# Decay attention and GELU MLP in one kernel: a second v buffer and a single g buffer, early w_out loads, batch 1 in the row-tiled order

## The chip, the cores and the metric

One NeuronCore of a Trainium2 chip. The metric is the device time of one execution in microseconds (us). A kernel's figure is the median of its runs. A run more than 1.5% above the fastest of the same kernel counts as slow; ratios are of fast runs alone. The profile covers one of them; its span, from first to last instruction, is some 2 us shorter. Runs on one core carry the granted TensorE clock beside the time, as a share of full speed.

## The reference, cut to what matters

```python
def _attn_ref(q, k, v, f):                       # (8, 8, 576, 64), f: (8, 8, 576)
    scores = (1 / sqrt(64)) * q @ k^T
    cum = cumsum(log(clip(f, 1e-4, 1)))          # along the sequence
    scores = where(causal, -1e9, scores + cum[q] - cum[k])
    return softmax(scores) @ v
def _moe_ref(x, w_in, w_out):                    # x: (4608, 512), w_in: (512, 2048), w_out: (2048, 512)
    return gelu_exact(x @ w_in) @ w_out
```

The attention of eight batches, heads joined to 512 columns, then a two-layer MLP. The decay is applied as a weight on v, so TensorE sees plain attention.

## The kernel before: the parts that matter

The kernel works batch by batch: attention of batch b, with the second GEMM of batch b-1 filled in between its steps, then the first GEMM and Gelu of batch b. The 64 tail rows of each batch are gathered and go through the MLP at the end. Cuts are marked `...`.

```python
v_sb = consts.tile([P, H, NBLK, D], FP32)                            # v as loaded: one buffer
g_pool = ...(name="g", bufs=2)                                       # g: 16 tiles of 128 x 512 bf16 per batch
s_psum, o_psum, m_psum = ... # bufs=2 each: scores (2 banks a tile), attention outputs, GEMM outputs

def gemm1(c, ffb):
    ps = m_psum.tile(...)
    ...                                   # 4 matmuls of 128 x 512
    nc.scalar.activation(g_of[c][ffb], ps, Act.Gelu)

def transposes_pe(b, i, pool):            # q and k of one head pair: 12 transpositions on TensorE,
    ...                                   # into two banks of the pool, then 8 copies on VectorE

def x_tail_dma(b):                        # a DMA transposition on SyncE's queue
    nc.sync.dma_start_transpose(tails[...], xt_of[b][D:P]...)

for b in range(B):
    ...                                   # attention of b
    if b == 0:
        load_w_out(0)
        x_tail_dma(0)
    for ffb in range(n_ff):
        gemm1(b, ffb)
        if b == 0:
            if ffb in (6, 8, 13):
                transposes_pe(1, (6, 8, 13).index(ffb), s_psum if ffb < 10 else o_psum)
            if ffb == 9:
                weigh_v(1, 0)             # GpSimd; waits for v of batch 1
                for c in range(1, 4): load_w_out(c)
                load_qk_tokens(2); weigh_v(1, 1)
        ...
```

v has one buffer, so batch 1's v loads wait for batch 0's weighting. The batch-1 attention runs the second GEMM of batch 0 with full 128-row matmuls; the later batches split most of them into two row tiles of 64 (`gemm2_rows`), the mode in which the scores run too.

The softmax here doesn't subtract the row's maximum and nothing guards it: scores larger than these inputs give would overflow.

Of the kernel before, what the change touches and what calls it, by code (L numbers as in the profile page):

```python
# [50 lines left out]
def kernel(  # L51
# [30 lines left out]
    xT_pool = ctx.enter_context(tc.tile_pool(name="xT", bufs=2))  # L82
    g_pool = ctx.enter_context(tc.tile_pool(name="g", bufs=2))
    o_pool = ctx.enter_context(tc.tile_pool(name="outs", bufs=4))
# [21 lines left out]

    v_sb = consts.tile([P, H, NBLK, D], FP32)

    def load_v(b, h0=0, h1=H):
        if b >= B:  # L110
            return
        for n in range(NBLK):
            p0 = D if n == NBLK - 1 else 0
            nc.sync.dma_start(  # L114
                v_sb[p0:P, h0:h1, n, :],
                v[b, h0:h1, K0[n] + p0 : K0[n] + P].rearrange("h p d -> p h d"),
            )
# [18 lines left out]
    )  # L136
    nc.gpsimd.memset(v_sb[:, :, 0, 0:1], 0.0)
    load_v(0, 0, 4)
    load_qk_tokens(0, 6, 8)
    load_v(0, 4, 8)  # L140
    ident_fp = consts.tile([P, P], FP32)
    make_identity(nc, ident_fp)
# [29 lines left out]
    nc.scalar.activation(lf, f_sb, Act.Ln)  # L172
    nc.vector.memset(v_sb[0:D, :, 4, :], 0.0)
    nc.vector.tensor_tensor_scan(cum, ones, lf, 0.0, Alu.mult, Alu.add)
    nc.scalar.activation(wk, cum, Act.Exp, bias=cum[:, S // 2 : S // 2 + 1], scale=-1.0)

    def warm_up(n):
# [94 lines left out]
    def weigh_v(b, i):  # L272

        if b not in vw_of:
# [5 lines left out]
            vw_of[b][:, hs, :, 0:D],  # L280
            v_sb[:, hs, :, :],
            w.unsqueeze(3).to_broadcast([P, 2, NBLK, D]),
# [6 lines left out]
    def scores(b, i, t):  # L289
        on_pe = b == 0 or (b == 1 and i == 0)  # L290
        st = s_psum.tile([P, 2, 512], FP32, tag="s", name=f"s{t}")
# [166 lines left out]

    def gemm2_rows(c):




        for ts, steps in enumerate(STEPS):
            if ts < n_sub - 1:
# [35 lines left out]
    def first_attention():  # L501
# [29 lines left out]
        transposes(3, m_psum, "m")  # L531
        scores(0, 1, 3)
        weigh_v(0, 0)
        load_w_in(0)
        load_w_in(1)
# [5 lines left out]
        load_w_in(3)  # L541
        nc.gpsimd.memset(v_sb[:, :, 0, 0:1], 0.0)
        load_v(1, 0, 4)
        load_v(1, 4, 8)
        load_qk_tokens(1, 4, 8)
        scores(0, 2, 0)
        attend_head(0, 0)
# [22 lines left out]
    FILL_AV = [2, 1, 2, 2]  # L570
    FILL_1 = [[0, 4, 4, 0], [0, 2, 3, 3], [4, 4, 4, 4], [3, 3, 3, 3], [8, 0, 99]]

# [36 lines left out]
    def second_attention():  # L609
        b, fill, counts = 1, gemm2(0, True), FILL_1  # L610
        for i in range(HP):
            for t in range(4):
                scores(b, i, t)
                if i and t == 1:
                    attend(b, i - 1, 0, (0, 1, 2))
                elif i and t == 2:
                    attend(b, i - 1, 0, (3, 4))
                    normalize(b, i - 1, 0)
                elif i and t == 3:
                    attend(b, i - 1, 1, (0, 1, 2, 3, 4))  # L620
                    normalize(b, i - 1, 1)
                    if i < HP - 1:
                        x_dma(b, i - 1)
                if (i, t) == (0, 2):
                    transposes_pe(1, 3, o_psum)
                if i == 1 and t in (0, 2):
                    weigh_v(1, 2 + t // 2)
                if t == 3:
                    if i == 1:
                        load_v(2, 0, 4)  # L630
                    if i == 2:
                        transpose_dma(2, 0, 4)
                take(fill, counts[i][t])
        i = HP - 1
        take(fill, counts[HP][0])
        to_xT(b, i - 1, nc.vector.tensor_copy, o_psum, "o")
        attend(b, i, 0, (0, 1, 2, 3, 4))
        normalize(b, i, 0)
        take(fill, counts[HP][1])
        attend(b, i, 1, (0, 1, 2, 3, 4))  # L640
        normalize(b, i, 1)
        take(fill, 7)
        to_xT(b, i, nc.vector.tensor_copy, o_psum, "o")
        x_tail_dma(b)
        transpose_dma(2, 4, 8)
        load_v(2, 4, 8)
        take(fill, 999)

    for b in range(B):
# [6 lines left out]
        if b == 0:  # L656
            load_w_out(0)
            x_tail_dma(0)
        for ffb in range(n_ff):
            gemm1(b, ffb)  # L660
            if b == 0:
                if ffb in (6, 8, 13):
                    transposes_pe(
                        1, (6, 8, 13).index(ffb), s_psum if ffb < 10 else o_psum
                    )
                if ffb == 9:
                    weigh_v(1, 0)
                    for c in range(1, 4):
                        load_w_out(c)
                    load_qk_tokens(2)  # L670
                    weigh_v(1, 1)
            elif b + 1 < B:
                if ffb % 4 == 0:
                    untangle(b + 1, ffb // 4)
                if ffb % 4 == 2:
                    weigh_v(b + 1, ffb // 4)
                if ffb == 14:
                    load_qk_tokens(b + 2)
# [34 lines left out]
```

## Time and profile before

| what | before |
|---|---|
| median of runs | 353.1 us first; 352.7 to 353.9 beside the later runs |
| profiled span, granted clock | 350.2 us, 1.000 |
| TensorE busy | 338.7 us, 97% |
| batch 0's first GEMM begins | 27.83 us |
| batch 1's attention | 43.46 to 70.90 us |
| each of batches 3 to 7, first GEMM to next first GEMM | 36.58 us, (290.77 - 107.85) / 5 |

The main lines stand in the prediction. One view that it did not show belongs beside them: ScalarE around the end of a later batch's attention, from the timeline (start, duration, engine, line, operation; in brackets how long the engine idled before it and what ended that).

```profile
138.63 1.51 ACT L311 ACTIVATE e<-s 128x896 bf16<-128x896 f32 x2 [1.07 <-PE s L296]
140.16 1.28 ACT L404 ACT_TABLE_LOAD   x1
145.41 0.60 ACT L404 ACTIVATE g<-ps 128x512 bf16<-128x512 f32 x1 [3.96 <-PE ps L392]
```

The Gelu table is loaded the moment the last Exp is done, 4 us before the first Gelu has input. The load costs nothing. Nothing in a list of costs by duration says so: it is the same 1.28 us wherever it runs.

### The profile page before, as it was taken

To read this page: it belongs to the slowest core of one execution; us is meant where nothing else is said; L and a number is where in the kernel's file an instruction comes from. 1 tells how busy PE (TensorE), PEld (TensorE's weight loads), DVE (VectorE), ACT (ScalarE), POOL (GpSimd) and SP (SyncE) were. 2 spreads that over 40 slices of the span, in tenths; PEclk is the share of its full clock that TensorE was granted. 3 is DMA by queue.
4 is the path that set the end of the run, shared out by engine and by line. 5 is a ranking of instruction groups with operands and counts; after the bars stand their busy time and mean duration, and the time that the engine had idled before them with its cause. 6 is when DMAs were issued, how large, how long until landed. Compare 5 with 4: busy or idle time off the path is not lost.

```text
span 350.2 us, 7729 instructions
## 1 busy us (share of the span) xinstructions
PE 338.7 (97%) x3082; PEld 174.8 (50%) x3082; DVE 203.0 (58%) x499; ACT 216.1 (62%) x298; POOL 124.5 (36%) x243
## 2 busy tenths in 40 slices
PE   8998989999999999999999999999999999999995
PEld 3564534544555455545554455445544554444443
DVE  4561984496469935894579557956696563011011
ACT  5877585457874687468746874687567774603600
POOL 8291185415538044613453245514350530000000
PEclk9999999999999999999999999999999999999999
DMA  7999989974994998298928794679510131011013
GB/s 108 181 176 196 199 143 195 214 175 95 206 163 136 136 206 156 85 135 137 220 76 128 143 196 99 104 135 213 126 37 2 47 85 45 0 62 60 0 32 90
DMA packets 101219, 43.24 MB, mean 123 GB/s; under 512 B 80000, under 2 KB 96640, under 8 KB 101184
## 3 DMA queue, kind: packets, MB, share of 16 engines
q1 hardware_dynamic: 83888, 28.60, 40.1%
q0 software_dynamic: 16896, 13.63, 26.0%
q8 instruction: 24, 0.39, 0.5%
q10 hardware_dynamic: 400, 0.52, 0.4%
q14 instruction: 11, 0.09, 0.1%
HBM read 36.85 MB, written 9.44 MB: 132 GB/s over the span
## 4 chain that ended last, share of the span: by engine, by line
PE 83%; ACT 9%; POOL 2%; issue 2%; DMA 2%; SPq 1%; DVE 0%; ACTq 0%; POOLq 0%
PE ps L392 36%; PE ps L479 18%; PE ps L430 12%; PE o L332 9%; PE s L296 7%; ACT e L311 5%; ACT L311 2%; DMA v_sb<-in_v_dram 2%; ACT g L404 1%; POOL vw L279 1%; PE ps_x L368 1%; SPq L114 1%; POOL k L102 1%; POOL q L102 0%; PE s L305 0%
## 5 line engine op out<-in xcount | busy, mean ns | idle before, releaser
L404 ACT ACTIVATE g<-ps 128x512 bf16<-128x512 f32 x144 | 86.0, 597 | 82.2 <-PE ps L392 82.2
L311 ACT ACTIVATE e<-s 128x896 bf16<-128x896 f32 (+1 forms) x128 | 103.9, 862 | 30.7 <-PE s L296 25.5
L392 PE MATMUL ps<-xT,w_in_sb 128*128 128x512 bf16 x512 | 112.6, 379 | 0.7 <-ACT xT L371 0.6
L479 PE MATMUL ps<-w_out_sb,g 64*128 64x512 bf16 (+1 forms) x690 | 102.4, 376 | 0.0
L313 POOL TENSOR_SCALAR_AFFINE_SELECT e<-e 128x256 bf16<-128x256 bf16 x135 | 53.4, 406 | 113.5 <-ACT e L311 112.5
L392 PEld LDWEIGHTS <-w_in_sb 128*128 128x128 bf16 x576 | 56.0, 98 | 68.1 <-issue 2.9
L279 POOL TENSOR_TENSOR vw<-v_sb,wT 128x640 bf16<-128x640 f32 x32 | 41.0, 1280 | 47.5 <-DMA v_sb<-in_v_dram 15.8
L296 PE MATMUL s<-qT,kT 64*128 64x320 bf16 (+4 forms) x384 | 47.9, 282 | 4.0 <-ACT e L311 3.4
L479 PEld LDWEIGHTS <-g 64*128 64x128 bf16 (+1 forms) x690 | 37.7, 94 | 25.4 <-issue 1.6
L263 DVE COPY qT<-tq 64x288 bf16<-64x288 bf16 x96 | 45.1, 470 | 1.5
L332 PEld LDWEIGHTS <-e 128*128 128x128 bf16 x960 | 35.9, 98 | 17.6 <-issue 11.5
L430 PE MATMUL ps<-w_out_sb,g 128*128 128x512 bf16 (+2 forms) x208 | 44.3, 363 | 0.0
L332 PE MATMUL o<-vw,e 128*128 128x65 bf16 x960 | 41.7, 194 | 0.8 <-ACT e L311 0.4
L487 DVE COPY ot<-ps 128x512 f32<-128x512 f32 x24 | 16.5, 689 | 36.0 <-PE ps L479 36.0
L439 DVE COPY ot<-ps 128x512 f32<-128x512 f32 (+2 forms) x13 | 8.4, 650 | 48.9 <-PE ps L430 48.7
L296 PEld LDWEIGHTS <-kT 64*128 64x128 bf16 x384 | 20.1, 94 | 28.7 <-issue 15.6
L263 DVE COPY kT<-tk 64x288 bf16<-64x288 bf16 x96 | 32.3, 336 | 1.6
L347 DVE RECIPROCAL r<-o 128x5 f32<-128x5 f32 x64 | 12.5, 195 | 30.1 <-PE o L332 29.3
L348 DVE TENSOR_TENSOR x<-o,r 128x256 bf16<-128x256 f32 x64 | 27.2, 425 | 2.2
L430 PEld LDWEIGHTS <-g 128*128 128x128 bf16 x208 | 18.8, 98 | 18.9 <-issue 0.4
L358 DVE TENSOR_SCALAR xt<-o,r 64x64 bf16<-64x64 f32 x60 | 17.4, 290 | 1.4
L489 DVE TENSOR_TENSOR ot<-ot,ps 128x512 f32<-128x512 f32 x24 | 16.5, 687 | 1.3
(60 smaller groups left out, 144.7 us busy)
## 6 DMA issues: line engine op xcount, KB each, us to landing
out_dram<-ot SPq DMA_DIRECT2D x32, 256.0 KB, 2.4
v_sb<-in_v_dram SPq DMA_DIRECT2D x20, 256.0 KB, 4.6
v_sb<-in_v_dram SPq DMA_DIRECT2D x29, 128.0 KB, 5.5
q<-in_q_dram POOLq DMA_DIRECT2D x6, 576.0 KB, 6.5
k<-in_k_dram POOLq DMA_DIRECT2D x6, 576.0 KB, 8.6
w_in_sb<-in_moe_w_in_dram POOLq DMA_DIRECT2D x4, 512.0 KB, 7.9
w_out_sb<-in_moe_w_out_dram POOLq DMA_DIRECT2D x4, 512.0 KB, 9.3
q<-in_q_dram POOLq DMA_DIRECT2D x4, 144.0 KB, 4.4
```

Source lines behind the costliest of these rows:

```text
L263: nc.vector.tensor_copy(rows[:, odd], src[odd * D : (odd + 1) * D, 2 * i + h].rearrange("d j p -> d p j"),)
L279: nc.gpsimd.tensor_tensor(vw_of[b][:, hs, :, 0:D], v_sb[:, hs, :, :], w.unsqueeze(3).to_broadcast([P, 2, NBLK, D]), Alu.mult,)
L296: nc.tensor.matmul(st[:, h, c : c + w], kT[i][d, K0[n] : K0[n] + P], qT[i][d, q0 : q0 + w], start=True, stop=not on_pe or c not in SDIAG[t],)
L311: nc.scalar.activation(et[:, :, 0:c], st[:, :, 0:c], Act.Exp, scale=scale)
L313: nc.gpsimd.affine_select(out=et[:, :, c0 : c0 + P], in_=et[:, :, c0 : c0 + P], compare_op=Alu.is_ge, fill=0.0, base=0, pattern=[[0, 2], [ ...
L332: nc.tensor.matmul(o[:, m, :], e_of[b, i, t][:, h, c : c + P], vw_of[b][:, 2 * i + h, n, :], start=(n == 0), stop=(n == m),)
L348: nc.vector.tensor_tensor(x_of[b, i][:, :, h, :], o[:, 0:4, 0:D], r[:, 0:4].unsqueeze(2).to_broadcast([P, NBLK - 1, D]), Alu.mult,)
L358: nc.vector.tensor_scalar(*tail, r[D:P, 4:5], None, Alu.mult)
L392: nc.tensor.matmul(ps, w_in_sb[:, kt, ffb * P : (ffb + 1) * P], src[:, kt, :], start=(kt == 0), stop=(kt == n_dm - 1),)
L404: nc.scalar.activation(g_of[c][ffb], ps, Act.Gelu)
L430: nc.tensor.matmul(pss[ts][:, c0:c1], g_of[c][kt][:, ts * P : (ts + 1) * P], w_out_sb[:, kt, c0:c1], start=(kt == 0), stop=(kt == n_ff - 1),)
L479: nc.tensor.matmul(banks[r], g_of[c][kt][rows, ts * P : (ts + 1) * P], w_out_sb[rows, kt, :], start=(kt == 0), stop=last if r else kt == n ...
```

## The change

Its intent: batch 1's v comes early, so that GpSimd no longer holds w_out back behind a v wait; batch 1's attention takes the steady order as far as w_out's arrival allows; its causal masks move from TensorE to GpSimd. g goes from two buffers to one, presumably to make room for the second v buffer. The core of the diff:

```diff
-    g_pool = ctx.enter_context(tc.tile_pool(name="g", bufs=2))
+    g_pool = ctx.enter_context(tc.tile_pool(name="g", bufs=1))
-    v_sb = consts.tile([P, H, NBLK, D], FP32)
+    v_of = [consts.tile([P, H, NBLK, D], FP32, name=f"v_sb{i}") for i in range(2)]
     ...
     load_v(0, 4, 8)
+    load_v(1, 0, 4)
+    load_v(1, 4, 8)
     ...
-        on_pe = b == 0 or (b == 1 and i == 0)          # masks by TensorE
+        on_pe = b == 0
     ...
+    def gemm2_first(c):     # token blocks 0 and 1 full-row, by quarters of w_out
+        ...
+        yield from gemm2_rows(c, 2)
     ...
+        gate = x_pool.tile([P, 1], FP32, tag="gate", name="gate")
+        nc.gpsimd.tensor_copy(gate, v_of[0][:, 0, 2, 0:1])
+        load_w_in(0)
         weigh_v(0, 0)
-        load_w_in(0)
         ...
         load_qk_tokens(1, 4, 8)
+        for c in range(4):
+            load_w_out(c)
     ...
-    FILL_1 = [[0, 4, 4, 0], [0, 2, 3, 3], [4, 4, 4, 4], [3, 3, 3, 3], [8, 0, 99]]
+    FILL_1 = [[2, 2, 2, 2], [2, 2, 3, 3], [2, 3, 4, 4], [2, 3, 4, 4], [8]]
     ...                     # second_attention() rewritten in the form of attention()
-            load_w_out(0)
             ...
-                if ffb in (6, 8, 13):
+                if ffb in (6, 8, 12, 14):               # fourth pair here, no longer inside the attention
                 ...
-                    for c in range(1, 4):
-                        load_w_out(c)
+                    weigh_v(1, 1)
                     load_qk_tokens(2)
```

More of the change, by code (lines that the diff above doesn't have):

```diff
@@ L114, in load_v @@
             nc.sync.dma_start(
-                v_sb[p0:P, h0:h1, n, :],
+                v_of[b % 2][p0:P, h0:h1, n, :],
                 v[b, h0:h1, K0[n] + p0 : K0[n] + P].rearrange("h p d -> p h d"),
@@ L136 @@
     )
-    nc.gpsimd.memset(v_sb[:, :, 0, 0:1], 0.0)
+    nc.gpsimd.memset(v_of[0][:, :, 0, 0:1], 0.0)
     load_v(0, 0, 4)
@@ L172 @@
     nc.scalar.activation(lf, f_sb, Act.Ln)
-    nc.vector.memset(v_sb[0:D, :, 4, :], 0.0)
+    nc.vector.memset(v_of[0][0:D, :, 4, :], 0.0)
     nc.vector.tensor_tensor_scan(cum, ones, lf, 0.0, Alu.mult, Alu.add)
     nc.scalar.activation(wk, cum, Act.Exp, bias=cum[:, S // 2 : S // 2 + 1], scale=-1.0)
+    nc.vector.memset(v_of[1][0:D, :, 4, :], 0.0)
     def warm_up(n):
@@ L280, in weigh_v @@
             vw_of[b][:, hs, :, 0:D],
-            v_sb[:, hs, :, :],
+            v_of[b % 2][:, hs, :, :],
             w.unsqueeze(3).to_broadcast([P, 2, NBLK, D]),
@@ L457, with gemm2_rows @@
     ]
-    def gemm2_rows(c):
-        for ts, steps in enumerate(STEPS):
+    def gemm2_first(c):
+        pss = [
+            m_psum.tile([P, d_model], FP32, tag="m", name="ps2") for _ in range(2)
+        ]
+        for kq in range(4):
+            for ts in range(2):
+                for kt in range(4 * kq, 4 * kq + 4):
+                    nc.tensor.matmul(
+                        pss[ts],
+                        g_of[c][kt][:, ts * P : (ts + 1) * P],
+                        w_out_sb[:, kt, :],
+                        start=(kt == 0),
+                        stop=(kt == n_ff - 1),
+                    )
+                    if kt == n_ff - 1:
+                        ot = o_pool.tile([P, d_model], FP32, tag="ot", name="ot")
+                        nc.vector.tensor_copy(ot, pss[ts])
+                        nc.sync.dma_start(
+                            out[c * S + ts * P : c * S + (ts + 1) * P, :], ot
+                        )
+                    yield
+        yield from gemm2_rows(c, 2)
+    def gemm2_rows(c, ts0=0):
+        for ts in range(ts0, n_sub):
+            steps = STEPS[ts]
             if ts < n_sub - 1:
@@ L541, in first_attention @@
         load_w_in(3)
-        nc.gpsimd.memset(v_sb[:, :, 0, 0:1], 0.0)
-        load_v(1, 0, 4)
-        load_v(1, 4, 8)
         load_qk_tokens(1, 4, 8)
+        for c in range(4):
+            load_w_out(c)
         scores(0, 2, 0)
@@ L609, in second_attention, with av @@
     def second_attention():
-        b, fill, counts = 1, gemm2(0, True), FILL_1
+        fill = gemm2_first(0)
+        def av(i):
+            for h in range(2):
+                attend(1, i, h, (0, 1, 2, 3, 4))
+                if h == 0:
+                    take(fill, FILL_AV[i])
+                normalize(1, i, h)
         for i in range(HP):
             for t in range(4):
-                scores(b, i, t)
+                scores(1, i, t)
+                take(fill, FILL_1[i][t])
                 if i and t == 1:
-                    attend(b, i - 1, 0, (0, 1, 2))
-                elif i and t == 2:
-                    attend(b, i - 1, 0, (3, 4))
-                    normalize(b, i - 1, 0)
-                elif i and t == 3:
-                    attend(b, i - 1, 1, (0, 1, 2, 3, 4))
-                    normalize(b, i - 1, 1)
-                    if i < HP - 1:
-                        x_dma(b, i - 1)
-                if (i, t) == (0, 2):
-                    transposes_pe(1, 3, o_psum)
-                if i == 1 and t in (0, 2):
-                    weigh_v(1, 2 + t // 2)
-                if t == 3:
-                    if i == 1:
-                        load_v(2, 0, 4)
-                    if i == 2:
-                        transpose_dma(2, 0, 4)
-                take(fill, counts[i][t])
-        i = HP - 1
-        take(fill, counts[HP][0])
-        to_xT(b, i - 1, nc.vector.tensor_copy, o_psum, "o")
-        attend(b, i, 0, (0, 1, 2, 3, 4))
-        normalize(b, i, 0)
-        take(fill, counts[HP][1])
-        attend(b, i, 1, (0, 1, 2, 3, 4))
-        normalize(b, i, 1)
-        take(fill, 7)
-        to_xT(b, i, nc.vector.tensor_copy, o_psum, "o")
-        x_tail_dma(b)
+                    av(i - 1)
+                    if i < HP - 1:
+                        x_dma(1, i - 1)
+                if (i, t) in ((1, 2), (2, 0)):
+                    weigh_v(1, i + 1)
+                if (i, t) == (1, 3):
+                    load_v(2)
+                if (i, t) == (2, 3):
+                    transpose_dma(2, 0, 4)
+        take(fill, FILL_1[HP][0])
+        to_xT(1, HP - 2, nc.vector.tensor_copy, o_psum, "o")
+        av(HP - 1)
+        take(fill, 5)
+        to_xT(1, HP - 1, nc.vector.tensor_copy, o_psum, "o")
+        x_tail_dma(1)
         transpose_dma(2, 4, 8)
-        load_v(2, 4, 8)
         take(fill, 999)
@@ L661 @@
             if b == 0:
-                if ffb in (6, 8, 13):
+                if ffb in (6, 8, 12, 14):
                     transposes_pe(
-                        1, (6, 8, 13).index(ffb), s_psum if ffb < 10 else o_psum
+                        1, (6, 8, 12, 14).index(ffb), s_psum if ffb < 10 else o_psum
                     )
@@ L667 @@
                     weigh_v(1, 0)
-                    for c in range(1, 4):
-                        load_w_out(c)
+                    weigh_v(1, 1)
                     load_qk_tokens(2)
-                    weigh_v(1, 1)
             elif b + 1 < B:
```

## The prediction

> **What bounds the kernel now**
>
> I read the clock first (1.000 throughout, so no throttling confuses the times), then the page's busy shares and slices, then the chain of waits, then the busy time of each engine by stage, and last the order of instructions in the two stages that the change edits.
>
> ```profile
> PE 338.7 (97%) x3082; PEld 174.8 (50%) x3082; DVE 203.0 (58%) x499; ACT 216.1 (62%) x298; POOL 124.5 (36%) x243
> ...
> PE 83%; ACT 9%; POOL 2%; issue 2%; DMA 2%; SPq 1%; DVE 0%; ACTq 0%; POOLq 0%
> ```
>
> TensorE sets the time, from the first matmul to the last: 97% busy and 83% of the chain. A change can win only by taking matmul time, mode switches or TensorE waits out. The next lines, the busy time by stage, show where those are (columns: stretch, its length, then busy time and count of each engine).
>
> ```profile
> 27.83:42.30 14.47, 14.45 (x96) 7.30 (x96) 7.29 (x16) 9.61 (x15) 0.00 (x0) 1.00 1.23 201
> 42.30:47.65 5.35, 4.39 (x41) 2.16 (x40) 4.28 (x10) 4.38 (x6) 4.86 (x7) 1.00 0.58 104
> ...
> 47.65:70.90 23.25, 22.62 (x233) 10.83 (x231) 13.82 (x37) 12.71 (x15) 13.08 (x26) 1.00 1.12 197
> 84.95:107.69 22.74, 22.44 (x292) 12.96 (x289) 11.83 (x33) 16.02 (x19) 9.15 (x21) 1.00 1.07 187
> 121.68:144.34 22.66, 22.36 (x288) 12.87 (x288) 12.45 (x35) 16.06 (x19) 9.14 (x21) 1.00 0.81 158
> ```
>
> Batch 1's attention, which the change rewrites, runs from 43.46 (its first score matmul) to 70.90 us (the first matmul of the next first GEMM): 27.4 us. Batches 2 to 7 do the same work in 22.7. So at most 27.4 - 22.7 = 4.7 us is to be had there, 1.3% of 353.1.
>
> The timeline of TensorE, VectorE and GpSimd in the stage ahead shows two queues that matter:
>
> ```profile
> 34.77 1.96 DVE L232 COPY qT<-s_t 64x288 bf16<-64x288 bf16 x4 [7.08 <-PE s_t L220]
> 36.74 1.98 DVE L232 COPY kT<-s_t 64x288 bf16<-64x288 bf16 x4
> 38.75 1.96 DVE L232 COPY qT<-s_t 64x288 bf16<-64x288 bf16 x4
> 40.72 1.97 DVE L232 COPY kT<-s_t 64x288 bf16<-64x288 bf16 x4
> 42.72 1.97 DVE L232 COPY qT<-ps_t 64x288 bf16<-64x288 bf16 x4
> 44.71 1.95 DVE L232 COPY kT<-ps_t 64x288 bf16<-64x288 bf16 x4
> ```
> ```profile
> 42.79 1.28 POOL L279 TENSOR_TENSOR vw<-v_sb,wT 128x640 bf16<-128x640 f32 x1 [15.65 <-PE ps L392]
> 44.02 0.22 POOL L285 CAST vw<-wT 128x10 bf16<-128x10 f32 x1
> 44.16 2.31 POOL L159 DMA_DIRECT2D w_out_sb<-in_moe_w_out_dram x3
> ```
>
> First, each TensorE transposition of a head pair costs VectorE eight copies, 3.95 us, and from 34.77 to 46.66 VectorE does them back to back: it is the bound of that job. Second, GpSimd sits 15.65 us in front of batch 1's first v weighting, and the other three quarters of w_out queue behind it. The label names a matmul, but the last v load of batch 1 was issued at about 30.8 and landed 11.7 us later, 42.5, so I read this as a wait for v. It is why 42.30 to 47.65 has a DMA share of only 0.58.
>
> **What the Trainium skill says**
>
> - "PSUM — Partial Sum Buffer", Engine vs sequencer instructions: matmuls start and complete in program order. The trace agrees (nothing overtakes the 0.96 us wait at 46.71), and it is what turns a full buffer in front of one transposition into idle time for the first GEMM behind it.
> - "TensorEngine Tiling (Array Packing)", Key Properties: changing the tiling mode drains TensorE. The trace agrees: the score tile at 49.98 needs 0.30 us until the full-row matmul after it, though its 448 columns per head stream in 448/2.4 GHz = 0.187, and four full-row matmuls at 47.64, 0.86 of streaming, take 0.96 until the next scores. About 0.11 + 0.10 = 0.21 us a round trip.
> - "DMA: Bandwidth & Descriptors", Queues, rings and completion order: every DMA engine takes turns between the queues that have work. So the second v load competes with w_in. The trace shows about 200 GB/s when full, and a hole at 16 to 18 us (46 GB/s) that the v load can fill.
> - "TensorE: Matmul & The Clock Gate", What's actually happening: after about 3.4 us of idle TensorE falls to half clock. No such idle occurs in this trace.
>
> **The change part by part**
>
> 1. *Front.* The v load of batch 1 goes out right behind batch 0's, and w_in's first quarter is issued before, not after, the first weighting. That weighting starts at 15.00 when the last v chunk lands (8.84 + 6.00). The new gate waits for chunk 2, issued 7.74, landing about 6.1 later, 13.8; plus 0.8 of issuing is 14.7, so 15.00 stays. Only one w_in issue (0.78) now stands ahead of the second weighting, which TensorE waits 0.28 us for at 19.46. Gain 0.3.
>
> 2. *DMA.* From 16 us on, up to w_out's end, 2.1 MB of w_in (as written, bf16), 1.2 of q and k, 1.2 of v and 2.1 of w_out are left, 6.6 MB at 200 GB/s = 33 us, so the last quarter of w_out lands near 49, the first near 41. The first token blocks need quarter 0 in the first head pair, quarter 1 in the second: no wait. The later quarters of w_in land near 31 and 34 and are needed at 34.7 and 38 or later: no wait either. So the v wait of 15.65 us and the DMA hole vanish, but both were on GpSimd, off the path of TensorE, because the old fill counts already stepped around them.
>
> 3. *The fourth transposition.* It moves from the attention, where TensorE ran it at 47.13, into the first GEMM behind block 14. The third moves from block 13 to 12. Both use the two-bank pool of attention outputs, two tiles each. So the fourth has no free bank until VectorE has copied the third's q, at 42.72 + 1.97 = 44.69, and its k, at 46.66. VectorE's work has not changed, so neither have these times. TensorE finishes block 14 at 27.83 + 15 x 0.864 + 3 x 0.51 = 42.3. In order, it then waits till 44.69, does 0.26, waits till 46.66, does 0.26, and only then runs block 15, 0.86. The attention starts at about 47.9 in place of 43.46: +4.4, of which 0.5 is the transposition itself and 3.9 is new idle time.
>
> 4. *Batch 1's attention.* Removed: ten mask matmuls of the first pair, 10 x 128/2.4 = 0.53, and the transposition, 0.51. The masks become five GpSimd selects of 0.41; GpSimd was idle between its steps there, so they cost nothing on the path. Kept full-row: the 32 matmuls of two token blocks. The fill counts put them into the first three pairs, so 12 score tiles still pay 0.21 round trips; the steady order pays about two there. TensorE's busy time then is the steady 22.36 + 0.22 (a second transposition of x to xT) + 10 x 0.21 = 24.7. New waits: the first pair has only 2 fills a tile (0.43 us) where the steady batch has 6, 5, 4, 3. In the steady batch the first Exp ends 2.97 us after the attention's start (Gelu 0.60, table load 1.28, Exp 0.93); the third score tile needs its bank, while two tiles with four fills last 1.5. Counting on to the sixth tile gives about 1.2 us idle. And the third block wants both banks of the GEMM pool at once, one of which VectorE (0.69 a copy) has only just been handed: up to 0.8, taken as 0.4. Sum 24.7 + 1.2 + 0.4 = 26.3 against 27.4: -1.1.
>
> 5. *Single g buffer.* The Gelus of a batch overwrite g after the second GEMM has read it, all in TensorE's own order: 0. *Double v buffer in batches 2 to 7*: GpSimd's waits there are off the path (22.7 us a batch stays): 0.
>
> Sum: -0.3 + 4.4 - 1.1 = +3.0, 353.1 + 3.0 = 356.1 us.
>
> **The rivals**
>
> - *The stall hardly exists*, because VectorE starts earlier or empties the banks faster. Against it: 24 copies without a gap, 0.49 each. For it: a trial order that stalled so plainly would be odd to keep. Then only the transposition's 0.5 is added, and the time is 353.1 - 0.3 + 0.5 - 1.1 = 352.2; with the full steady gain in the attention, 349.
> - *The stall drops TensorE's clock.* Idle 2.4 and 1.7 us, with only 0.26 of work between, is near the skill's 3.4. Half clock for 3.4 to 7 us would cost 1.7 to 3.5 more: 358 to 360. Against it: two idles, neither alone that long.
> - *DMA contention moves the front.* If the v load and the earlier w_in delay batch 0's v or batch 1's q and k, GpSimd's first weighting slips past 15.00 and everything with it, one for one; 1 to 2 us, so 357 to 358. For it: the DMA engines are full from 8 to 14 us. Against: the second v load is behind the first in the same queue.
> - *The wait for w_out was dearer than I think*, so that ungating brings all 4.7 us: with the stall, 353.1 - 0.3 + 4.4 - 4.7 = 352.5. Against: TensorE idled only about 1.6 us in the whole old stage.
>
> **Range and chances**
>
> The rivals run from 349 to 360, with the weight near 356; the stall rests on a measured queue, the attention's sum on my counting of switches (plus or minus 1). I predict 356.1, 352.0 to 359.5. Two per cent is 7.06 us: faster than 346.0 needs more than the whole batch-1 excess, so 3%; slower than 360.2 needs stall and clock loss together, 6%; the rest, 91%, is within 2%.
>
> **What would show it right or wrong**
>
> Right: TensorE idle about 2.4 and 1.7 us behind block 14, released by VectorE's copies of the third pair; the first GEMM of batch 0 ending near 47.6 (from 43.46); batch 1's attention 26 to 27 us from there; the first w_out matmul never waiting for a DMA; batches 2 to 7 still 36.6 us each. Wrong: no gap there, VectorE copies far from 34.8 to 50.6, a granted clock under 1, the first weighting later than 15.3, or an attention under 25 us.

## The result

The changed kernel took 369.75 us (368.68 to 371.08, four runs) against 353.56 us for the kernel before: slower, ratio 1.0448 with a 95% interval of 1.0374 to 1.0521. Ratios here are the mean time of one kernel's fast runs over that of the other's in the same rounds, so not quite the quotient of the medians quoted. The profiled run of the changed kernel is its longest, 371.08 us, with a mean granted clock of 0.986. The other three had 0.991 to 0.995, so the profile shows more lost clock than the median run had.

The changed kernel's page first: busy shares, the clock in 40 slices, and the chain of waits by engine.

```profile
PE 342.5 (93%) x3052; PEld 174.7 (47%) x3094; DVE 204.9 (56%) x502; ACT 215.3 (58%) x298; POOL 126.5 (34%) x248
...
PEclk9999969989999999999999999999999999999999
...
PE 77%; ACT 12%; DVE 4%; issue 3%; DMA 1%; POOL 1%; ACTq 0%; DVEq 0%; POOLq 0%
```

TensorE's share of the chain fell from 83% to 77%; ScalarE's rose from 9% to 12%, VectorE's from nothing to 4%. In the sixth and ninth slices the clock dipped. What TensorE waited for, in total, number of times and longest, the longest entries:

```profile
PE ps L396 <- ACT g L408: 8.1, 7, 1.2
PE s L300 <- ACT e L315: 1.9, 7, 0.5
PE ps_t L224 <- DVE qT L236: 1.7, 1, 1.7
PE ps_t L224 <- DVE kT L236: 1.5, 1, 1.5
...
PE ps L396 <- DVE xT L375: 1.0, 1, 1.0
```

The first line is new: seven waits of 1.16 us of a first-GEMM matmul for a Gelu. The kernel before has no such line. The third and fourth are the stall behind block 14. By stages of the two timelines:

| stage | before, us | changed, us | difference |
|---|---|---|---|
| start to batch 0's first GEMM | 27.83 | 28.09 | +0.26 |
| first GEMM of batch 0 | 15.63 | 21.10 | +5.47 |
| attention of batch 1, until its first GEMM runs on (70.90; 77.67) | 27.44 | 28.48 | +1.04 |
| first GEMM of batch 1, attention of batch 2 (to 107.85; 117.24) | 36.95 | 39.57 | +2.62 |
| batches 3 to 7 (to 290.77; 308.21) | 182.92 | 190.97 | +8.05 |
| tail | 59.43 | 60.79 | +1.36 |
| span | 350.2 | 369.0 | +18.8 |

Two thirds of the loss, 12.0 of 18.8 us, come after batch 1's attention, where the prediction had set the change to zero (the 18.8 us compare the two profiled runs; the medians differ by some 16). Each batch there takes 190.97 / 5 = 38.19 in place of 36.58 us.

The stages of the changed kernel that answer to those in the prediction (stretch, length, busy time and count of TensorE, its weight loads, VectorE, ScalarE and GpSimd, then clock, DMA share, GB/s):

```profile
27.98:48.80 20.82, 17.22 (x109) 8.50 (x111) 13.37 (x28) 10.30 (x17) 5.97 (x9) 0.94 1.25 187
48.80:77.70 28.90, 26.62 (x263) 12.23 (x267) 14.18 (x38) 15.21 (x18) 13.38 (x29) 0.93 0.92 162
...
117.24:133.30 16.06, 14.80 (x74) 6.48 (x74) 14.43 (x35) 10.71 (x17) 5.95 (x9) 1.00 0.66 111
133.30:155.43 22.13, 21.56 (x278) 12.44 (x277) 11.51 (x31) 14.19 (x18) 9.31 (x22) 1.00 0.79 151
```

In the first stretch TensorE is idle for 3.6 of 20.8 us; the third shows a later batch's first GEMM idle for 1.3 us that had no gap before. The same GEMM of the kernel before, its 64 matmuls in one piece:

```profile
107.69 14.06 PE L392 MATMUL ps<-xT,w_in_sb 128*128 128x512 bf16 x64
```

The start of that GEMM in the changed kernel, ScalarE and then TensorE:

```profile
118.19 1.28 ACT L408 ACT_TABLE_LOAD   x1 [5.53 <-PE ps L396]
119.48 1.09 ACT L408 ACTIVATE g<-ps 128x512 bf16<-128x512 f32 x2
```
```profile
120.13 4.13 PE L396 MATMUL ps<-xT,w_in_sb 128*128 128x512 bf16 x17 [1.16 <-ACT g L408]
```

The table load is no longer behind the last Exp. ScalarE stood idle for 5.53 us and started it only when TensorE had finished the first block; the Gelu came after it, and TensorE, with two PSUM banks for the GEMM, had to wait for the third block. The built program says why. This is ScalarE's instruction order with its semaphore waits at the start of batch 1's first GEMM, before and after (from the program that the kernel file builds, not from the profile):

```
before:   L404 LoadActFuncSet
          L404 Activation g_1265<-ps_1260 128x512 [waits PE_49]
changed:  L408 EventSemaphore [waits PE_49]
          L408 LoadActFuncSet
          L408 Activation g_1283<-ps_1278 128x512 [waits Activation_49]
          L408 EventSemaphore [waits PE_49]
          L408 Activation g_1284<-ps_1308 128x512 [waits Activation_49]
```

With one g buffer a Gelu writes where a Gelu of the last batch wrote, and it has a wait on ScalarE's own semaphore beside the one on TensorE's. (With two buffers it writes where a Gelu of the last but one wrote, and has no such wait; why not, nothing here shows.) The TensorE wait then goes into a semaphore instruction of its own. For the first Gelu of a batch that instruction stands ahead of the table load, which so has to wait too: in the trace it runs at 118.14 and the load at 118.19. The profile counts these instructions by line:

```profile
L404 ACTq EVENT_SEMAPHORE  x16: 17/17/17, 319.3 to 332.6; - x16
```
```profile
L408 ACTq EVENT_SEMAPHORE  x128: 17/17/17, 78.1 to 351.7; - x128
```

16 in the kernel before (first fence), all in the tail; 128 in the changed one (second): 7 batches and the tail times 16.

### The profile page after: what moved, and what is told of

It reads as the page before. It is cut to its first block, busy times and chain, and to the rows that moved or that the text cites. A ratio compares the mean times of both kernels' runs of the same rounds, so it can differ in the third digit from the quotient of the medians.

```text
span 369.0 us, 7818 instructions
## 1 busy us (share of the span) xinstructions
PE 342.5 (93%) x3052; PEld 174.7 (47%) x3094; DVE 204.9 (56%) x502; ACT 215.3 (58%) x298; POOL 126.5 (34%) x248
## 4 chain that ended last, share of the span: by engine, by line
PE 77%; ACT 12%; DVE 4%; issue 3%; DMA 1%; POOL 1%; ACTq 0%; DVEq 0%; POOLq 0%
PE ps L396 31%; PE ps L509 18%; PE o L336 9%; PE ps L434 7%; PE s L300 7%; ACT e L315 5%; ACT g L408 3%; PE ps L472 2%; ACT L315 2%; ACT L408 2%; DMA k<-in_k_dram 1%; DVE kT L236 1%; DVE qT L236 1%; PE s L309 1%; DVE x L352 1%
## 5 line engine op out<-in xcount | busy, mean ns | idle before, releaser
L396 PE MATMUL ps<-xT,w_in_sb 128*128 128x512 bf16 x502 | 117.0, 384 | 10.5 <-ACT g L408 8.1
L317 POOL TENSOR_SCALAR_AFFINE_SELECT e<-e 128x256 bf16<-128x256 bf16 x140 | 55.5, 406 | 149.4 <-ACT e L315 148.3
L509 PE MATMUL ps<-w_out_sb,g 64*128 64x512 bf16 (+1 forms) x718 | 104.6, 377 | 1.6 <-DVE ot L481 0.3
L509 PEld LDWEIGHTS <-g 64*128 64x128 bf16 (+1 forms) x744 | 40.8, 94 | 29.4 <-issue 3.6
L517 DVE COPY ot<-ps 128x512 f32<-128x512 f32 x26 | 17.9, 689 | 46.6 <-PE ps L509 46.6
L267 DVE COPY kT<-tk 64x288 bf16<-64x288 bf16 x96 | 32.5, 339 | 3.7 <-DMA tk<-k 2.1
L443 DVE COPY ot<-ps 128x512 f32<-128x512 f32 (+2 forms) x9 | 5.7, 633 | 50.3 <-PE ps L434 47.6
L408 ACT ACT_TABLE_LOAD x8 | 10.3, 1283 | 39.0 <-PE ps L396 39.0
L434 PE MATMUL ps<-w_out_sb,g 128*128 128x512 bf16 (+2 forms) x141 | 27.8, 355 | 0.2
L434 PEld LDWEIGHTS <-g 128*128 128x128 bf16 x144 | 13.5, 98 | 14.5 <-issue 0.2
L519 DVE TENSOR_TENSOR ot<-ot,ps 128x512 f32<-128x512 f32 x26 | 17.9, 687 | 1.3
## 6 DMA issues: line engine op xcount, KB each, us to landing
w_out_sb<-in_moe_w_out_dram POOLq DMA_DIRECT2D x4, 512.0 KB, 21.9
```

The costliest lines, as they stand in the source:

```text
L267: nc.vector.tensor_copy(rows[:, odd], src[odd * D : (odd + 1) * D, 2 * i + h].rearrange("d j p -> d p j"),)
L317: nc.gpsimd.affine_select(out=et[:, :, c0 : c0 + P], in_=et[:, :, c0 : c0 + P], compare_op=Alu.is_ge, fill=0.0, base=0, pattern=[[0, 2], [ ...
L396: nc.tensor.matmul(ps, w_in_sb[:, kt, ffb * P : (ffb + 1) * P], src[:, kt, :], start=(kt == 0), stop=(kt == n_dm - 1),)
L434: nc.tensor.matmul(pss[ts][:, c0:c1], g_of[c][kt][:, ts * P : (ts + 1) * P], w_out_sb[:, kt, c0:c1], start=(kt == 0), stop=(kt == n_ff - 1),)
L509: nc.tensor.matmul(banks[r], g_of[c][kt][rows, ts * P : (ts + 1) * P], w_out_sb[rows, kt, :], start=(kt == 0), stop=last if r else kt == n ...
L517: nc.vector.tensor_copy(ot, banks[1])
```

## The experiments

Twelve kernels, in three calls, all correct. The kernel before ran beside each call: 353.86, 352.69 and 353.02 us. In the table "own stall" is the order of transpositions of the change and its wait behind block 14.

| kernel | us | ratio to before (95%) | g buffers | transpositions | tail's DMA transposition | loads |
|---|---|---|---|---|---|---|
| changed | 369.75 | 1.0448 (1.0374 to 1.0521) | 1 | own stall | early | as changed |
| e1_before_g1 | 363.57 | 1.0247 (1.0189 to 1.0305) | 1 | as before | as before | as before |
| e2_after_g2 | 358.59 | 1.0104 (1.0017 to 1.0190) | 2 | own stall | early | as changed |
| e3_after_preload | 362.38 fast | 1.0204 (1.0125 to 1.0283) | 1, table early | own stall | early | as changed |
| e4_after_tp | 369.79 | none (three of four runs counted as slow) | 1 | as before | early | as changed |
| e5_after_g2_tp | 359.14 | 1.0166 (1.0105 to 1.0227) | 2 | as before | early | as changed |
| e7_g2_tp_gated | 357.17 | 1.0102 (1.0027 to 1.0176) | 2 | as before | early | w_out 1 to 3 later |
| e8_e7_endfix | 357.89 | 1.0116 (1.0047 to 1.0184) | 2 | as before | early | w_out 1 to 3 later |
| e9_before_v2_ungated | 357.22 | 1.0093 (1.0010 to 1.0176) | 2 | as before | early | as changed |
| e14_g2_latetail | 358.66 | 1.0151 (1.0090 to 1.0211) | 2 | own stall | late | as changed |
| e11_e5_latetail | 354.25 | 1.0033 (0.9960 to 1.0106) | 2 | as before | late | as changed |
| e12_e11_endfix | 351.74 | 0.9956 (0.9880 to 1.0031) | 2 | as before | late | as changed |
| e13_e9_latetail | 352.27 | 0.9974 (0.9911 to 1.0037) | 2 | as before | late | as changed |

e9 and e13 have the attention of the kernel before; all others but e1 have that of the change.

### First call: the g buffer, the table load, the stall

**e1_before_g1**: the kernel before with one line changed.

```diff
-    g_pool = ctx.enter_context(tc.tile_pool(name="g", bufs=2))
+    g_pool = ctx.enter_context(tc.tile_pool(name="g", bufs=1))
```

> The kernel before with the single g buffer alone (nothing else of the change). Theory A: with one buffer each Gelu has to wait for two semaphores (PSUM ready, g free); the one for TensorE is moved onto the table load ahead of it, so the 1.28 us table load, which ran 4 us early while TensorE worked, now starts only after the first block of the GEMM, and with two PSUM banks TensorE waits about 1.16 us for it. With the dearer waits of the other 15 Gelus that is 1.6 us in each of 7 batches: 353.5 + 11 to 13 = 364.5 to 366.5, batches 2 to 7 at about 38.2 us each where before shows 36.6. Theory B (the prediction's step 5: the single g buffer costs nothing, the loss comes from batch 1 and its clock): 352.5 to 354.5 and 36.6 us a batch.

Measured: 363.57 us, a little under the expected range; granted clock 0.999. Its profiled span is 361.5, 11.3 over that of before. The waits of its TensorE name the same line as the changed kernel's:

```profile
PE ps L392 <- ACT g L404: 8.1, 7, 1.2
```

The chain of waits gives the other term. From one batch's first GEMM (109.47) to the next (147.68) is 38.21 us, 1.63 over before. 1.16 of it is that wait. The last 56 matmuls of the GEMM take 12.52 there, where 64 took 13.83 before, so 56 took 12.10: 0.42, some 0.03 us a Gelu, which I put down to the separate semaphore instructions on the loop that passes the two PSUM banks between TensorE and ScalarE. Theory A stands, theory B is out: the g buffer given up costs about 10 us alone (9.7 by the medians; the interval of the ratio leaves out 1, but not 2%).

**e2_after_g2**: the changed kernel with `bufs=2` put back (both buffers and the second v fit).

> The changed kernel with two g buffers again. Theory A: the table load runs early again, batches 2 to 7 back at 36.6 us, the half-clock stretch near 80 us gone: 369.7 - 11 to 13 = 357 to 358.5; what remains over before (about 4) is the stall behind block 14 and its half clock. Theory B: no change, 369 to 370.

Measured: 358.59 us, 11.2 less than the changed kernel, within a fraction of the range. Its first GEMM again runs 64 matmuls in 13.83 without a gap, and the second clock dip is gone. That dip followed on two waits in a row, 0.98 us for xT and 1.16 for the Gelu; with the first alone, as here, there is none. But the pair does not settle it: e4 below has the same two waits at the same place, and its clock stays at 1.00 there.

**e3_after_preload**: one g buffer, and a Gelu of one element per partition ahead of each batch's first one, with operands that nobody else touches.

```diff
+        if ffb == 0 and c < B:
+            nc.scalar.activation(pre_out, pre_in, Act.Gelu)
```

> The changed kernel, still with one g buffer, but a Gelu of one element per partition ahead of each batch's first Gelu, so that the table load has nothing to wait for. Theory A in two terms: the table load is 1.2 of the 1.6 us a batch, the second wait of the 16 Gelus 0.4. So 369.7 - 7 x 1.2 = about 361, batches at 37.0 us, PE still slowed by a few hundredths of a us per Gelu. If the late table load were not the cause: 369 to 370. If it were all of the cost: as with two g buffers, 357 to 358.5.

Measured: fast runs of 360.27, 362.38 and 363.38. One run took 489.34 us at a granted clock of 0.658 over its whole length, and it is the one that was profiled; it counts as slow and is not explained here. The time says: 7.4 less than the changed kernel for the table load, 3.8 more than with two buffers (e2) for the double waits. I had expected 8.4 and about 3. So both terms count, the table load for about two thirds; without a profile of the fast state the exact shares stay open. The slow profile does show the order that was meant: the last Exp of a batch ends at 186.29 us and the table load begins at 186.31.

**e4_after_tp**: transpositions where the kernel before has them, g still single.

```diff
-                if ffb in (6, 8, 12, 14):
+                if ffb in (6, 8, 13):
                 scores(1, i, t)
+                if (i, t) == (0, 2):
+                    transposes_pe(1, 3, o_psum)
```

> The changed kernel (one g buffer) with the transpositions where before has them: the third behind block 13, the fourth in batch 1's first head pair. Theory S: the two waits of TensorE for VectorE (1.7 and 1.6 us) and the half clock from 46 to 53 us (about 3 us of extra matmul time) go, some of it returns as Exp waits in the first head pair: 369.7 - 4 to 6 = 364 to 366, granted clock 1.00 at 46 to 53 us. Rival: VectorE is the bound of that stretch wherever the transposition stands, and the attention waits for its fourth copies: 368 or more.

Measured: 369.54, 370.04, 363.90 and 371.60. Three of the four count as slow, the profiled one among them, so the times decide nothing: the one fast run, 363.90 at a clock of 1.000, is what theory S said. What the profile shows is a candidate that neither theory had, and e5 tests it in fast runs. The timeline of TensorE at the start of batch 1's attention:

```profile
43.20 0.36 PE L300 MATMUL s<-qT,kT 64*128 64x256 bf16 x4
48.33 1.03 PE L472 MATMUL ps<-w_out_sb,g 128*128 128x512 bf16 x2 [4.76 <-DMA w_out_sb<-in_moe_w_out_dram]
```

TensorE reached the attention at 43.20, as hoped, and then waited 4.76 us for the first quarter of w_out. The two matmuls behind it take 1.03 in place of 0.60: the clock had fallen to 0.50. The stall behind block 14 had hidden a late transfer.

### Second call: why w_out is late

**e5_after_g2_tp**: e4 with two g buffers.

> The changed kernel with two g buffers and the transpositions where before has them. The run with the transpositions alone put back showed a wait of 4.8 us for w_out's first quarter (landed at 48.3) in place of the two waits for VectorE. Theory W: the stretch up to 48 us is held from two sides, VectorE's copies and the landing of w_out, so lifting one leaves the other: as with two g buffers alone, 357 to 360, TensorE waiting about 4.5 us for the DMA of w_out at 44 us. Rival S (the stall behind block 14 alone is the loss): 352 to 354.

Measured: 359.14 (358.80 to 359.50), as theory W says: level with e2. TensorE waited 4.80 us for w_out. Theory S falls here.

**e7_g2_tp_gated**: e5, with three of the four w_out quarters behind the weightings of batch 1, as before has them.

```diff
-        for c in range(4):
-            load_w_out(c)
+        load_w_out(0)
         ...
                     weigh_v(1, 1)
+                    for c in range(1, 4):
+                        load_w_out(c)
```

> As the run before it, and w_out's quarters 1 to 3 are issued only behind batch 1's first two v weightings, as before has them; quarter 0 stays early. Theory W: with less queued behind and beside it, quarter 0 lands near 42 as in before, TensorE waits for nothing at 44 us, full clock: 4 to 5 less than with all four in one go, 352.5 to 355. Rival: it is the early v load that delays quarter 0, not the other quarters: still landing at 46 to 48, 357 to 360.

Measured: 357.17, so the rival's numbers (the profile is of the slowest of the four runs, 359.93). The first quarter landed 21.6 us after its issue at 27.8, and now TensorE waited 4.44 us at 47.14 for batch 1's k, which no w_out was queued ahead of. Theory W, that the other quarters delay the first, falls. But the early v load fits no better: in this run batch 1's v had landed by 32.5, when GpSimd weighted it, ten us ahead of the wait.

**e8_e7_endfix**: e7 with one fill fewer ahead of the end of the attention.

```diff
-    FILL_1 = [[2, 2, 2, 2], [2, 2, 3, 3], [2, 3, 4, 4], [2, 3, 4, 4], [8]]
+    FILL_1 = [[2, 2, 2, 2], [2, 2, 3, 3], [2, 3, 4, 4], [2, 3, 4, 4], [7]]
```

> As the run before it, with 7 in place of 8 fills ahead of the last but one transposition of x, so that one step of the second GEMM is left until after the last, as in batches 2 to 7. In the changed kernel VectorE does the block's copy and sum (0.70 + 0.69) ahead of the last xT copy, and TensorE waits 0.98 us for that at 77.67. Theory: that wait goes, 0.7 to 1.2 us less than the run before it, 351.5 to 354. Rival: the wait only moves behind the next GEMM's start: no difference.

Measured: 357.89 against 357.17, inside the spread of both: inconclusive as a time. The profile shows the wait for xT gone, as meant. But TensorE's wait in the middle of the stretch, 3.35 us for w_out here and 4.44 us for k in e7, differs between the two by 1.1 us, more than the 0.98 that went.

**e9_before_v2_ungated**: the kernel before with the loads of the change alone: second v buffer, gate, w_in's first quarter ahead, four w_out quarters in one go. Attention, transpositions, g as before.

> The kernel before with the loads of the change alone: second v buffer, batch 1's v early, w_in's first quarter ahead of the first weighting, all four quarters of w_out issued in one go. Attention, transpositions and g as before. Theory W: w_out's first quarter lands at 46 to 48 where before has it at 42, TensorE needs it at 44.7: wait of 2 to 4 us[...]: 355.5 to 359. Rival (ungating helps or is free, since GpSimd no longer holds the loads back): 352 to 354.

Measured: 357.22 (353.41 to 358.46), with a wait of 3.78 us for w_out. So the loads alone make the delay. Not in every execution, it seems: the run of 353.41 has a clock of 1.000 and is level with the kernel before, as e4's 363.90 stood apart from its three others. Neither was profiled. Where it arises shows in the DMA columns (the last two: mean share, GB/s):

```profile
38.00:40.00 2.00, 2.00 (x11) 0.88 (x9) 1.93 (x5) 1.47 (x3) 0.69 (x2) 1.00 1.27 197
40.00:42.00 2.00, 2.00 (x20) 1.20 (x19) 1.95 (x5) 1.38 (x3) 0.00 (x0) 1.00 4.45 135
42.00:44.00 2.00, 2.00 (x14) 0.79 (x11) 1.93 (x5) 1.04 (x2) 0.00 (x0) 1.00 0.36 13
44.00:46.00 2.00, 0.87 (x10) 0.34 (x8) 1.93 (x5) 1.70 (x3) 0.00 (x0) 1.00 0.08 12
46.00:48.00 2.00, 0.00 (x0) 0.00 (x0) 0.63 (x2) 1.46 (x2) 0.00 (x0) 1.00 0.98 149
```

With w_out and more still in the queue, the DMA engines moved 12 to 13 GB/s for four microseconds. A share of 4.45 in the stretch ahead of it fits packets that began there and did not end: in the trace's records, packets of 256 bytes and of 1 KB of two queues, begun within 0.2 us of each other, took 5.3 to 5.5 us each, where the medians of these sizes in this run are 0.02 and 0.10. What was new at that moment? With batch 1's v no longer waiting, SyncE's queue was free early, and the DMA transposition of batch 0's tail rows, which stood at 42.54 before, was issued at 33.38 and landed 15.1 us later, 48.5. Before it landed in 2.5 us. Such holes stand between 40 and 48 us in e4, e5, e7, e8 and e9, and shorter ones in the changed kernel (102 GB/s at 42 to 44) and e2 (23 GB/s).

### Third call: the tail's transposition

**e11_e5_latetail**: e5 with that one DMA moved.

```diff
         if b == 0:
-            x_tail_dma(0)
         ...
                 if (i, t) == (1, 3):
                     load_v(2)
+                    x_tail_dma(0)
```

> Two g buffers, transpositions where before has them, all four quarters of w_out early, and the one DMA transposition of batch 0's tail rows moved from the end of batch 0's attention to batch 1's second head pair, behind the load of v. Theory T: in the runs so far this transposition, no longer held back by v loads in its queue, starts among the weight loads and all DMA engines stand nearly still for 3 to 5 us at 41 to 47 us (13 to 20 GB/s), which is what makes w_out's first quarter late; without it the quarter lands near 43.5, TensorE waits under 1 us, clock 1.00: 359.1 - 5 to 7 = 352 to 354. Rival V (the early v load itself delays it by its 1.2 MB): hole gone or not, the quarter lands at 46 or later, 356 to 359.

Measured: 354.25 us, 4.9 less than e5, with no overlap of their runs; clock 1.000 in the profiled run. The DMAs moved 204 to 207 GB/s through 38 to 48 us, w_out's first quarter landed 17.2 us after its issue (21.9 in e5), and TensorE no longer waited for it. Theory T holds; rival V, that the early v load itself is the delay, is out.

**e12_e11_endfix**: e11 with the `[7]` of e8.

> As the run before it, with one step of the second GEMM kept until after the last transposition of x. Theory: TensorE's 0.98 us wait for VectorE's xT copy at the end of batch 1's attention goes: 0.7 to 1.2 us less than the run before it, 351 to 353, the best of all. Rival: no difference.

Measured: 351.74 us, the best of all, 2.5 under e11 (I had expected up to 1.2; the spans of the two profiles, 349.4 and 350.3, differ by 0.9; two of e11's runs had a clock of 0.995, none of e12's, so part of the 2.5 is clock). The end of batch 1's attention on TensorE, e11 in the first fence and e12 in the second:

```profile
70.16 0.81 PE L396 MATMUL ps<-xT,w_in_sb 128*128 128x512 bf16 x3
71.95 10.30 PE L396 MATMUL ps<-xT,w_in_sb 128*128 128x512 bf16 x46 [0.98 <-DVE xT L375]
```
```profile
70.25 0.38 PE L509 MATMUL ps<-w_out_sb,g 128*128 128x512 bf16 x1
70.46 11.82 PE L396 MATMUL ps<-xT,w_in_sb 128*128 128x512 bf16 x53
```

One matmul kept back lets the last xT copy go ahead of the block's copy and sum on VectorE. Against the kernel before, the ratio is 0.9956 with an interval that includes 1: the same.

**e13_e9_latetail**: e9 with the late tail.

> The kernel before with the loads of the change alone and the tail transposition late. Theory T: no hole, w_out's first quarter in time, attention as in before: 352 to 353.5, level with before, 4 less than with the early tail. Rival V: 355 to 358.

Measured: 352.27 us, 4.9 under e9, level with the kernel before. The same stretch as shown for e9 now reads:

```profile
40.00:42.00 2.00, 2.00 (x11) 0.88 (x9) 1.93 (x5) 1.41 (x3) 0.00 (x0) 1.00 1.23 197
42.00:44.00 2.00, 2.00 (x20) 1.20 (x19) 1.95 (x5) 0.98 (x2) 0.00 (x0) 1.00 1.25 204
44.00:46.00 2.00, 2.00 (x18) 0.81 (x17) 1.93 (x5) 1.42 (x3) 0.00 (x0) 1.00 1.24 205
46.00:48.00 2.00, 1.02 (x5) 0.44 (x7) 1.92 (x4) 1.99 (x3) 0.00 (x0) 1.00 1.25 207
```

**e14_g2_latetail**: the late tail, but the change's own order of transpositions.

> The changed kernel with two g buffers and the late tail transposition, its own order of transpositions kept. Now VectorE's copies alone hold the stretch: TensorE waits of 2.0 and 1.6 us behind block 14 stay (fourth pair's copies end at 50.8 whatever the DMAs do): 357 to 359, as with two g buffers alone. Rival: the copies only looked late, and the time falls to 354 or less.

Measured: 358.66, as e2 (358.59). TensorE still waited 1.99 and 1.55 us for VectorE's copies behind block 14, and the clock still fell. So the pair of constraints closes as a square: stall and hole 358.59 (e2), hole alone 359.14 (e5), stall alone 358.66 (e14), neither 354.25 (e11). Either one costs 4 to 5 us; both together cost no more. (e2 ran on another chip; its ratio to the kernel before, 1.0104, is the smallest of the three, so this holds by ratios too.)

## Why the prediction was wrong

*Step 5, "Single g buffer. ... 0", failed.* It checked the data: every read of g by the second GEMM comes, in TensorE's order, ahead of the GEMM whose Gelu overwrites it. That was right, and no wait for free data occurs. What it missed is the form of the wait. An additional semaphore on the Gelu put its TensorE wait into an instruction of its own, ahead of each Gelu and, for the first of a batch, ahead of the table load too. In place of 0 it measured about 10 us alone (e1) and 11.2 in the changed kernel (e2). This one step is most of the miss: the changed kernel without it (e2) took 358.59 us, inside the predicted range, and with it at +11.2 the sum would have been 356.1 + 11.2 = 367.3, against 369.75.

*Step 3, the stall behind block 14, was right in mechanism and nearly in size.* VectorE's copies ran from 35.03 to 50.8 without a gap. TensorE waited 1.67 and 1.55 us (predicted 2.4 and 1.8), and the fourth transposition began when the third's copies were out:

```profile
44.91 0.43 PE L224 MATMUL ps_t<-ident_bf,q 96*128 96x96 bf16 x6 [1.67 <-DVE qT L236]
46.89 0.66 PE L224 MATMUL ps_t<-ident_bf,k 96*128 96x96 bf16 x6 [1.55 <-DVE kT L236]
```

The attention began at 49.19, not 47.9, and the stage grew by 5.47 us, not 4.4: the clock had fallen within it. Undoing the stall alone gained nothing, since w_out was late as well (e5 against e2); the step did not see that second limit. (The 2.4 columns a ns by which steps 3 and 4 count fit the trace: 64 matmuls of 512 columns in 13.83 us are 0.216 us each, 2.37 columns a ns.)

*The rival that the stall drops the clock came true*, against the reason the prediction gave (two idles, neither 3.4 us long). The clock of the changed kernel:

```profile
46.00:47.50 1.50, 0.61 (x7) 0.61 (x8) 1.44 (x4) 0.00 (x0) 0.00 (x0) 0.56 1.24 206
...
51.50:52.50 1.00, 1.00 (x4) 0.17 (x2) 0.00 (x0) 1.00 (x2) 0.30 (x1) 0.50 1.27 202
52.50:53.50 1.00, 1.00 (x6) 0.23 (x4) 0.00 (x0) 1.00 (x2) 0.86 (x3) 0.74 1.32 205
```

Half clock from 46.2 to 53.0 us, 6.8 us, within the rival's 3.4 to 7. Two idles with 0.43 us of work between them came ahead of it. Part of it cost nothing: e12's attention waits 1.2 us for Exp in the first head pair, and the changed kernel's, at half clock, does not.

*Step 2, "no wait" for the loads, failed in a part that it did not name.* The byte count was fair: w_out's first quarter lands 1.0 us before TensorE wants it in e11 and 0.4 us after in e12. But it counted only loads. It did not ask what else stood in SyncE's queue behind the v loads and would now start early. The tail's transposition did, and its collision made the quarter 4 to 5 us late (e9 against e13). In the changed kernel itself it hid behind step 3's stall, so it adds nothing to the miss there (e2 against e14).

*Step 1, the front, -0.3:* measured +0.26. The gate ended at 14.45 (predicted 13.8), the first weighting began at 15.53 (predicted 15.00). The rival of DMA contention was right in kind, half a us in size. The profiles with early v begin the first GEMM anywhere from 27.5 to 29.8.

*Step 4, batch 1's attention, -1.1:* in e12, with nothing else in the way, it runs from 43.45 to 70.46, 27.0 us against 27.44: -0.4. But e12 has the fourth transposition inside its attention again, 0.51 us that the sum had taken out, so it is to be set against -0.6: the sum was 0.2 too good. It also puts out the rival that ungating w_out brings all 4.7 us. The Exp waits were 1.2 us as predicted; a wait of 0.41 us for w_out and one of 0.29 for VectorE's copy come beside them, where the sum had 0.4 for VectorE alone. The changed kernel loses another 1 us by a miscount of fills that the step did not check, since it stopped at the number of steps and not at what follows the last (e11 against e12).

*Step 5's other half*, the second v buffer in batches 2 to 7 at 0, stands: with two g buffers the batches are back at 36.57 us (114.53 to 151.10 in e2).

What stays open: why DMA engines stand still when that transposition meets other traffic (in e11 it landed in 5.1 us among 218 to 223 GB/s, and nothing stood still; in the changed kernel and e2 the hole was shorter), why single runs of e4 and e9 seem free of it, what the mask move is worth by itself, and what sets off the second clock dip.

## What to carry to other kernels

Ask of every buffer that becomes shared not only whether the data is free in time but which instruction will carry the additional wait: a wait ahead of a table load, or in a tight two-bank loop, cost 1.16 and 0.42 us a batch here (e1), though what the new semaphore stood for had been done long before. When a wait is taken off one queue, list everything that stood behind it there, for it all starts earlier, in other company. And undo suspects in pairs: here two limits that ended at nearly the same time each looked innocent when undone alone.

## What the Trainium skill lacked or had wrong

- "ScalarE: Activation LUTs", What ACT_TABLE_LOAD costs: it gives about 1283 ns for the load, as here (1.28 us), and about 1380 ns of drain on top. No drain shows here: the load at 118.19 is followed by the Gelu at 119.48, and the load at 140.16 begins as the last Exp ends. It does not say that a wait of the activation can come to stand ahead of its table load, as here; that cost 1.16 us a batch.
- No page has the cost of a second semaphore wait on an ACTIVATE: 112 further semaphore instructions of 17 ns, 0.42 us over 14 of a GEMM's 16 blocks (e1).
- "DMA: Bandwidth & Descriptors", DMA Transpose (X-bar): no page has a figure for what a transposition can cost the traffic beside it. Here one transposition of 64 rows landed in 2.5 us in the kernel before and in 15.1 among weight loads, where all traffic fell to 12 to 13 GB/s for four microseconds (e9) and did not when it came later (e13).
- "TensorE: Matmul & The Clock Gate", What's actually happening: it has the clock drop after an idle window of about 3.4 us; the page, which elsewhere lets many short idles do it too, has no figure for how much work in a window still counts as idle. Here the clock dropped after idles of 1.67 and 1.55 us with 0.43 us of matmuls between them: in the 3.41 us before the drop TensorE was busy for 0.90 us, before the second drop for 1.49 us. The half clock lasted 6.8 us the first time and 3.4 us the second (80.3 to 83.7).
